# A chunked RWKV-7 recurrence with a SoLU block: all chunk products on 64x64 blocks, paired evictions, two-block solve hops, and another order of loads

## The chip, the core and the metric

The kernel runs on one core of one Trainium2 chip. The metric is the device time of one execution in microseconds (us), lower is better. The core has TensorE (PE, matrix products, writes to PSUM only), VectorE (DVE), ScalarE (ACT), GpSimd (POOL) and SyncE (SP); SP and ACT, and in the changed kernel POOL too, issue DMA transfers. "PEld" in the profile is the weight load of TensorE.

## The reference

Two blocks follow one another. The first is a recurrence for 4 batches of 8 heads, 768 tokens and head width 40; the second is a feed-forward block on the result (3072 tokens of width 320).

```python
for t in range(S):                                   # per batch and head; state is 40 x 40
    y[t]  = r[t] @ state
    Sa    = state @ a[t]
    state = state * w[t][None, :] - outer(Sa, b[t]) + outer(v[t], k[t])
x  = y laid out as (batch, token) x (head, width)    # 3072 x 320
h  = x @ w_in                                        # 320 x 1024
e  = exp(h - max(h)); solu = h * e / (sum(e) + 1e-9)
ln = (solu - mean(solu)) / sqrt(var(solu) + 1e-6) * g_ln
out = ln @ w_out                                     # 1024 x 320
```

The recurrence's inputs are fp32. `w_in` and `w_out` arrive as 64-bit floats, which the kernel loads as pairs of 32-bit words and narrows to fp32 itself.

## The kernel before

**Tiling.** The 768 tokens are cut into chunks of 64. A step `i` of the main loop handles chunk `i // 2` of batch pair `i % 2`, so there are 24 steps; a tile has 128 partitions, 64 tokens of each of the two batches. Within a step a "unit" (p, g, q, h) is one batch half `p` and one head, given by three bits. Most products are made per unit, 16 of them, on 64 x 64 blocks of the PE array; `in_turn` deals the units over the blocks in turn, so that neighbours in the instruction stream use different blocks. A fp32 product shows as two records in the profile.

**What a step does.** `decay` takes the logarithm of `w` (`lw`), sums it over the chunk by products with a triangle (`pcum`, `pex`), and scales `b` and `k` (`kb`, on POOL, then to DRAM as `kb_dram`). `front` transposes `b` and `a` (`pbT`, `paT`; four 128-wide transposes each) to `bT` and `aT`. `norm` makes the strictly triangular matrix `nt` of each unit, and `spread` writes its 32 x 32 diagonal blocks, by way of DRAM, into a tile `blk` in which four steps fill the 128 partitions. `invert` inverts these blocks on DVE for four steps at once: 30 substitution steps of two operations (`prod`, `uu`), each dependent on the one before; it is a generator, from which `some(n)` draws at several places of the loop. `bring` loads the inverses as `tu` and `uh`. `couple` (product `py`, then `wy`) and `close` (product `pz`) make the off-diagonal block of the 64 x 64 inverse: the two hops of the solve. `attend` transposes `k`, `v`, `r` (`pkT`, `pvT`, `prT`), `states` the state (`psT`); each transposition is evicted by an ACT copy of its own. `scores` (`ps`) makes the masked tiles `psi` and `lv` of the next step on DVE. `carried` and `driven` (`px`) make the right-hand side, `solved` (`pu`) the solution, `answered` (`pl`) the masked tile `lu`, `read` (`pyo`) the outputs and the state's increment, `leave` the scaled outputs `x` (sent through DMA into `xT`) and the new state. The feed-forward block follows: `hidden` (`h`, its maximum `nmax`, the exponential `e`), `weighed`, `spreadof` (`bs`, `mv`, `c`, `rs`), `folded` (`plnT`) and `output` (`po`, `osb`).

**Order.** The loop (L660 to 704) runs the stages of different steps beside each other: in pass `i`, `decay` belongs to step i + 9, `front` to i + 8, `norm` to i + 7, `attend`, `couple`, `scores` and `close` to i + 1, `carried` to `leave` to i, `hidden` to i - 1 and `output` to i - 2. PE executes in the order in which the loop writes its instructions. The order on the other engines is decided by a scheduler when the kernel is built, from its own estimate of when each operand is ready; on the chip each engine then runs its list strictly in order. PSUM is used through a ring of six one-bank tiles (`bank`) and one two-bank tile for `h`; a new bank waits until the readers of the tile six places earlier are done.

**Weights.** `weights` is a generator from which the passes -4 to 0 draw. Its loads are issued from ACT's queue into two alternating tiles (`landing`), and each piece is narrowed by `narrow`: three operations on DVE for the bits, a clamp and the last product on POOL (L143, L152), two conversions on ACT (L144, L147) and two more operations on DVE (L149, L150). `w_out` pieces are also scaled by `g_ln` on POOL (L184); then a product `pmean` and a subtraction centre them.

Of the kernel before, what the change touches and what calls it, by code (L numbers as in the profile page):

```python
# [16 lines left out]
P = 128  # L17
# [28 lines left out]
def kernel(  # L46
# [34 lines left out]
    ps1 = ctx.enter_context(tc.tile_pool(name="ps1", bufs=6, space=PSUM))  # L81
    ps2 = ctx.enter_context(tc.tile_pool(name="ps2", bufs=1, space=PSUM))
    ctx.enter_context(tc.manual_schedule(engines={mybir.EngineType.PE}))
# [24 lines left out]
    a_t = zeroed(nc.vector, "a", [P, H, C], 3, pad)  # L108
# [5 lines left out]
    r_t = zeroed(nc.gpsimd, "r", [P, H, C], 2, pad)  # L114
    v_t = zeroed(nc.gpsimd, "v", [P, H, C], 2, pad)
# [12 lines left out]
    def bank(name):  # L128
        return ps1.tile([P, 512], FP32, tag="bank", name=name)


    def narrow(dst, bits):
# [4 lines left out]
        def tmp(name):  # L137
            return two.tile([P, 512], I32, tag=name, name="n_" + name)[0:n, 0:width]

        man, scale, low = tmp("psi"), tmp("s"), tmp("rT")  # L140
        ts = nc.vector.tensor_scalar
        ts(out=scale, in0=hi, scalar1=20, scalar2=0x7FF, op0=ALU.logical_shift_right, op1=ALU.bitwise_and)
        nc.gpsimd.tensor_scalar(out=scale, in0=scale, scalar1=1023 - 127, scalar2=1023 + 128, op0=ALU.max, op1=ALU.min)  # L143
# [8 lines left out]
        nc.gpsimd.tensor_tensor(out=dst, in0=frac, in1=scale.bitcast(FP32), op=ALU.mult)  # L152

    landing = ["e", "lnT"]

    def load_weight(dst, parts, step):
        n, width = dst.shape
        wide_ = parts[0].dtype != FP32
        to = dst
        if wide_:  # L160
            landing.reverse()
            to = two.tile([P, 512], I64, tag=landing[0], name="bits", bufs=1)[0:n, 0:width]
        row = 0
        for part in parts:
            nc.scalar.dma_start(out=to[row:row + part.shape[0]], in_=part)
            row += part.shape[0]
        yield
        if wide_:
            for lo in range(0, width, step):
                narrow(dst[:, lo:lo + step], to[:, lo:lo + step])  # L170
                yield

    def weights():
        nc.scalar.dma_start(out=g_rows, in_=moe_g_ln.rearrange("(c p) -> c p", p=P))
        for cols in (slice(0, 512), slice(512, 1024)):
            for kt in range(NK):
                yield from load_weight(w_in[0:D * len(TILE_HEADS[kt]), kt, cols],
                                       [moe_w_in[h * D:h * D + D, cols] for h in TILE_HEADS[kt]], 256)
        pg = bank("pg")
        nc.tensor.transpose(out=pg[:, 0:NF], in_=g_rows, identity=ident[0:NF, 0:NF])  # L180
        nc.scalar.copy(out=g_col, in_=pg[:, 0:NF])
        for c in range(NF):
            yield from load_weight(w2[:, c, :], [moe_w_out[c * P:(c + 1) * P, :]], DM)
            nc.gpsimd.tensor_scalar(out=w2[:, c], in0=w2[:, c], scalar1=g_col[:, c:c + 1],  # L184
                                    scalar2=None, op0=ALU.mult)
        t = bank("pmean")
        for c in range(NF):
            nc.tensor.matmul(t[:, 0:DM], lhsT=c_("mean"), rhs=w2[:, c, :], start=c == 0, stop=c == NF - 1)
        nc.vector.tensor_tensor(out=w2, in0=w2, in1=t[:, 0:DM].unsqueeze(1).to_broadcast([P, NF, DM]),
                                op=ALU.subtract)  # L190
        yield
# [8 lines left out]
    units = [(p, g, q, h) for g in range(2) for p in range(2) for q in range(2) for h in range(2)]  # L200
# [16 lines left out]
    def pair(t, j):  # L217
        return t[:, j:j + 2, :].rearrange("p a b -> p (a b)")[:, 0:W2]
# [10 lines left out]
    def load(x, ap, i):  # L229
        bp, ci = where_(i)  # L230
        for p in range(2):
            nc.sync.dma_start(out=x[half(p), :, 0:D],
# [6 lines left out]
    def load_keys(i):  # L239
# [3 lines left out]
        for n, ap in (("w", w), ("b", b), ("k", k), ("a", a)):  # L243
            x = a_t[i % 3] if n == "a" else two.tile([P, H, D], FP32, tag="raw_" + n, name="raw_" + n)
            d["raw_" + n] = x
            load(x, ap, i)

    def load_values(i):
# [3 lines left out]
        for n, ap in (("v", v), ("r", r)):  # L252
            d["raw_" + n] = two.tile([P, H, D], FP32, tag="raw_" + n, name="raw_" + n)
            load(d["raw_" + n], ap, i)

    def in_value_order(i):
        if not ok(i):
            return
        d = st[i]
        d["v"], d["r"] = v_t[i % 2], r_t[i % 2]  # L260
        d["lv"] = two.tile([P, H, W2], FP32, tag="lv", name="lv")
        for x, n in ((d["v"][:, :, 0:D], "raw_v"), (d["r"][:, :, 0:D], "raw_r"), (d["lv"][:, :, C:], "raw_v")):
            nc.gpsimd.tensor_copy(out=x.rearrange("p (h x) d -> p h x d", h=2),  # L263
                                  in_=d[n].rearrange("p (x h) d -> p h x d", h=2))


    def decay(i):
# [5 lines left out]
        t = bank("pcum")  # L273
        nc.tensor.matmul(heads(t[:, 0:DM]), lhsT=c_("cum"), rhs=lw[:, :, 0:D], start=True, stop=True)  # L274
        inv = two.tile([P, DM], FP32, tag="inv", name="inv", bufs=1)
        nc.scalar.activation(out=inv, in_=t[:, 0:DM], func=AF.Exp, scale=-1.0)  # L276
        t = bank("pex")
        for j in range(4):
            nc.tensor.matmul(t[0:W2, j * P:(j + 1) * P], lhsT=pair(lw, 2 * j), rhs=c_("cum"), start=True, stop=True)  # L279
        ex = d["ex"] = ex_t[i % (AHEAD + 3)]  # L280
        nc.scalar.activation(out=ex[0:W2, :, :, 1:].rearrange("p b j t -> p j b t"),
                             in_=t[0:W2].rearrange("p (j b t) -> p j b t", j=4, b=2), func=AF.Exp)
# [5 lines left out]
    def turned(name, src_, bufs=1, evict=True):  # L288
        t = bank("p" + name)
        for j in range(4):  # L290
            nc.tensor.transpose(out=t[0:W2, j * P:(j + 1) * P], in_=pair(src_, 2 * j), identity=ident)  # L291
        if not evict:
            return t
        o = two.tile([P, 4, P], FP32, tag=name, name=name, bufs=bufs)
        nc.scalar.copy(out=o[0:W2].rearrange("p j t -> p (j t)"), in_=t[0:W2])
        return o

    def front(i):
        if not ok(i):
# [3 lines left out]
        ex = d["ex"]  # L303
        d["bT"] = turned("bT", d["kbw"][:, H:, :])
        t = turned("aT", d["raw_a"], evict=False)
        aT = d["aT"] = two.tile([P, 4, P], FP32, tag="aT", name="aT", bufs=AHEAD + 2)
        nc.vector.tensor_tensor(out=aT[0:W2].rearrange("p j (b t) -> p j b t", b=2),
                                in0=t[0:W2].rearrange("p (j b t) -> p j b t", j=4, b=2),
                                in1=ex[0:W2, :, :, 0:C].rearrange("p b j t -> p j b t"), op=ALU.mult)

    def masked(dst, t):
        nc.vector.tensor_tensor(out=dst, in0=t, in1=tri.unsqueeze(1).to_broadcast([P, 4, C]), op=ALU.mult)  # L312

    def keyed(t, i, u):
        p, g, q, h = u
        return t[rows(h), 2 * g + q, p * C:p * C + C]

    def valued(t, i, u):
        p, g, q, h = u
        return t[rows(q), 2 * h + g, p * C:p * C + C]  # L320

    def norm(i):
# [3 lines left out]
        t = [bank("pnt") for _ in range(2)]  # L326
        for u in in_turn(lambda p, g, q, h: (h, p ^ h)):
            p, g, q, h = u
            j = 2 * g + q
            mm(t[h][half(p ^ h), j * C:j * C + C], keyed(d["bT"], i, u), keyed(d["aT"], i, u))  # L330
        nt = d["nt"] = two.tile([P, 2, 4, C], FP32, tag="nt", name="nt", bufs=AHEAD + 1)
        for h in range(2):
            masked(nt[:, h], t[h][:, 0:256].rearrange("p (j c) -> p j c", j=4))
        d["nt_dram"] = dram.tile([P, H, C], FP32, tag="nt_dram", name="nt_dram", bufs=3)
# [35 lines left out]
    def bring(i):  # L370
# [6 lines left out]
        for x in range(2):  # L377
# [4 lines left out]
            nc.sync.dma_start(out=d["uh"][hi],  # L382
                              in_=uu[at + 16 + 8 * x:at + 24 + 8 * x, :, Q:].rearrange("h s t -> s h t"))

    def fetch(i):
# [3 lines left out]
        d["kb"] = two.tile([P, 2 * H, C], FP32, tag="kbx", name="kbx")  # L389
        nc.sync.dma_start(out=d["kb"], in_=d["kb_dram"])  # L390

    def couple(i):
# [3 lines left out]
        t = [bank("py") for _ in range(2)]  # L396
        for u in in_turn(lambda p, g, q, h: p ^ h):
            p, g, q, h = u
            j, x = 2 * g + q, half(p ^ h)
            mm(t[h][x, j * Q:j * Q + Q], d["nt"][x, h, j], d["tu"][x, 4 * h + j, 0:Q])  # L400
        for h in range(2):
            nc.scalar.activation(out=wy[:, h, :, 0:Q], in_=t[h][:, 0:4 * Q].rearrange("p (j c) -> p j c", j=4),
                                 func=AF.Copy, scale=c_("neg_hi"))

    def close(i):
# [3 lines left out]
        t = [bank("pz") for _ in range(2)]  # L409
        for u in in_turn(lambda p, g, q, h: p ^ h):  # L410
            p, g, q, h = u
            j, x = 2 * g + q, half(p ^ h)
            mm(t[h][x, j * Q:j * Q + Q], wy[x, h, j], d["uh"][x, 4 * h + j])
# [321 lines left out]
```

## Time and profile before

| what | value |
|---|---|
| time, median of 3 runs | 818.68 us (818.12 to 820.93) |
| the profiled execution | 821.3 us, span from first to last instruction 819.5 us |
| mean granted TensorE clock | 0.863 of full speed |
| busy: PE, weight loads, DVE, ACT, POOL | 644.9, 480.8, 379.0, 239.8, 168.4 us |
| DMA | 84.31 MB in 224901 packets, 103 GB/s on average |
| `pu` of step 0, of step 2, of step 23 start at | 157.6, 206.6, 778.5 us |

The times in lines of the profile are microseconds from the start of the span. A busy engine is not necessarily the one that sets the end; the chain of waits and the timeline say which one does at a given place. The profiled execution is one run, and it took 2.6 us more than the median.

### The profile page before, as it was taken

Reading aid. Unit: us, or ns where it says so; the run is one execution under the profiler, and the core shown is the slowest. Engines: PE = TensorE matmul, PEld = TensorE weight load, DVE = VectorE, ACT = ScalarE, POOL = GpSimd, SP = SyncE. Lnnn points to the kernel's source line nnn. Section 1 sums busy time; section 2 is a strip of 40 time slices with the busy share of each in tenths; the row PEclk is TensorE's granted clock in tenths of the full one; section 3 lists DMA queues with packets and bytes.
Section 4 is the critical chain, followed back from the end, with each engine's and each line's share of the span. In section 5 each row is a group of like instructions: output and inputs, shape, how many; then the busy total and the mean of one; then the engine's idle time right before and its main releaser. Section 6 shows DMA issues by size and latency. Waiting matters only on the chain.

```text
span 819.5 us, 26810 instructions
## 1 busy us (share of the span) xinstructions
PE 644.9 (79%) x11545; PEld 480.8 (59%) x11545; DVE 379.0 (46%) x1048; ACT 239.8 (29%) x592; POOL 168.4 (21%) x237
## 2 busy tenths in 40 slices
PE   4505506778989989889889899798997877989894
PEld 3304404657757766667667667676765665666652
DVE  3563572478403692343954228822479133123322
ACT  3323102323324322433234334133321222223121
POOL 6664234313202211221022102301111110000000
PEclk8655756669989989999989999799997789899997
DMA  7546847364464545554625655265422412011000
GB/s 149 145 133 138 204 109 191 64 138 95 96 169 108 111 79 129 155 122 89 146 80 115 152 133 127 49 161 125 97 70 52 120 47 54 23 52 41 15 20 13
DMA packets 224901, 84.31 MB, mean 103 GB/s; under 512 B 206088, under 2 KB 213136, under 8 KB 224016
## 3 DMA queue, kind: packets, MB, share of 16 engines
q1 hardware_dynamic: 220272, 76.12, 40.4%
q10 hardware_dynamic: 4512, 6.48, 2.7%
q8 instruction: 91, 1.49, 0.7%
q14 instruction: 26, 0.21, 0.1%
HBM read 49.53 MB, written 29.10 MB: 96 GB/s over the span
## 4 chain that ended last, share of the span: by engine, by line
PE 46%; DVE 23%; DMA 15%; issue 5%; POOL 5%; ACT 3%; SPq 2%; ACTq 0%; DVEq 0%; POOLq 0%
PE h L592 14%; PE po L642 10%; DMA kbx<-kb_dram 7%; DVE prod L360 5%; DVE uu L362 5%; PE pz L211 3%; PE pyo L211 3%; DVE e L604 3%; DVE nmax L595 3%; PE py L211 3%; DVE bs L612 2%; DMA uu_dram<-uu 2%; PE pu L211 2%; POOL n_s L143 2%; ACT e L598 2%
## 5 line engine op out<-in xcount | busy, mean ns | idle before, releaser
L595 DVE TENSOR_REDUCE nmax<-h 128x1 f32<-128x1024 f32 x24 | 29.4, 1223 | 305.0 <-PE h L592 305.0
L592 PE MATMUL h<-w_in,xT 120*128 120x512 f32 (+1 forms) x288 | 135.8, 622 | 0.0
L642 PE MATMUL po<-w,lnT 128*128 128x320 f32 x384 | 115.4, 456 | 3.9 <-ACT lnT L633 3.9
L642 PEld LDWEIGHTS po<-w,lnT 128*128 128x128 f32 x384 | 75.7, 203 | 34.9 <-ACT lnT L633 5.4
L592 PEld LDWEIGHTS h<-w_in,xT 120*128 120x128 f32 (+1 forms) x288 | 55.0, 197 | 62.2 <-issue 61.1
L598 ACT ACTIVATE e<-h,nmax 128x1024 f32<-128x1024 f32 x24 | 26.8, 1116 | 147.5 <-DVE nmax L595 147.5
L360 DVE TENSOR_TENSOR prod<-blk,uu 128x30 f32<-128x30 f32 (+9 forms) x180 | 62.9, 350 | 6.0
L362 DVE TENSOR_TENSOR uu<-uu,prod 128x30 f32<-128x30 f32 (+9 forms) x180 | 61.5, 342 | 5.7
L291 PE MATMUL pkT<-cst,kbx 128*104 128x128 f32 x96 | 18.7, 330 | 45.5 <-DMA kbx<-kb_dram 42.7
L621 POOL TENSOR_TENSOR rs<-c,mhalf 128x1 f32<-128x1 f32 x24 | 13.4, 557 | 188.7 <-DVE c L620 135.6
L285 POOL TENSOR_TENSOR kb<-raw_b,inv 128x320 f32<-128x320 f32 x24 | 20.9, 869 | 151.4 <-ACT inv L276 131.1
L291 PE MATMUL pbT<-cst,kb 128*104 128x128 f32 x96 | 18.4, 323 | 39.5 <-POOL kb L285 39.5
L263 POOL COPY v<-raw_v 128x320 f32<-128x320 f32 x24 | 10.9, 456 | 179.8 <-DMA raw_v<-in_v_dram 179.7
L274 PE MATMUL pcum<-lw,cst 128*128 128x320 f32 x48 | 24.6, 605 | 24.6 <-ACT lw L272 14.7
L211 PE MATMUL pyo<-lv,kbx 64*64 64x104 f32 x768 | 42.2, 268 | 0.5 <-DVE lv L312 0.4
L211 PE MATMUL pyo<-lu,kbx 64*64 64x104 f32 x768 | 41.0, 261 | 0.8 <-DVE lu L312 0.5
L291 PEld LDWEIGHTS pkT<-cst,kbx 128*104 128x104 f32 x96 | 12.2, 154 | 50.0 <-issue 46.9
L644 ACT ACTIVATE osb<-po,rs 128x320 f32<-128x320 f32 x24 | 12.7, 527 | 94.5 <-PE po L642 94.5
L211 PE MATMUL py<-tu,nt 64*64 64x32 f32 x768 | 30.6, 227 | 8.2 <-DMA tu<-uu_dram 6.0
L279 PEld LDWEIGHTS pex<-cst,lw 128*104 128x104 f32 x192 | 32.8, 223 | 7.0 <-issue 4.1
L474 ACT COPY x<-px 128x160 f32<-128x160 f32 x48 | 11.7, 295 | 83.7 <-PE plnT L632 25.4
L291 PEld LDWEIGHTS pbT<-cst,kb 128*104 128x104 f32 x96 | 11.4, 149 | 41.8 <-POOL kb L285 40.5
(105 smaller groups left out, 1253.1 us busy)
## 6 DMA issues: line engine op xcount, KB each, us to landing
kb_dram<-kb SPq DMA_DIRECT2D x24, 512.0 KB
kbx<-kb_dram SPq DMA_DIRECT2D x24, 512.0 KB
nt_dram<-nt SPq DMA_DIRECT2D x24, 256.0 KB
uu_dram<-uu SPq DMA_DIRECT2D x6, 1024.0 KB
raw_w<-in_w_dram SPq DMA_DIRECT2D x48, 80.0 KB
raw_b<-in_b_dram SPq DMA_DIRECT2D x48, 80.0 KB
raw_k<-in_k_dram SPq DMA_DIRECT2D x48, 80.0 KB
a<-in_a_dram SPq DMA_DIRECT2D x48, 80.0 KB
```

Of the source, the lines that this page charges most:

```text
L211: nc.tensor.matmul(o, lhsT=lhsT, rhs=rhs, start=start, stop=stop, skip_group_check=True)
L274: nc.tensor.matmul(heads(t[:, 0:DM]), lhsT=c_("cum"), rhs=lw[:, :, 0:D], start=True, stop=True)
L279: nc.tensor.matmul(t[0:W2, j * P:(j + 1) * P], lhsT=pair(lw, 2 * j), rhs=c_("cum"), start=True, stop=True)
L285: nc.gpsimd.tensor_tensor(out=kb[:, j * H:j * H + H, 0:D], in0=d["raw_" + n], in1=heads(inv), op=ALU.mult)
L291: nc.tensor.transpose(out=t[0:W2, j * P:(j + 1) * P], in_=pair(src_, 2 * j), identity=ident)
L360: nc.vector.tensor_tensor(out=t, in0=nb[:, j:j + 1, j + 1:Q].to_broadcast([P, j, m]), in1=u[:, 0:j, j:j + 1].to_broadcast([P, j, m]), op=A ...
L362: nc.vector.tensor_tensor(out=u[:, 0:j, j + 1:Q], in0=u[:, 0:j, j + 1:Q], in1=t, op=ALU.subtract)
L592: nc.tensor.matmul(h[:, hh], lhsT=d["xT"][0:n, kt, :], rhs=w_in[0:n, kt, hh], start=kt == 0, stop=kt == NK - 1)
L595: nc.vector.tensor_reduce(out=nmax, in_=h, axis=AX.X, op=ALU.max, negate=True)
L598: nc.scalar.activation(out=e, in_=h, func=AF.Exp, bias=nmax, accum_out=d["esum"])
L604: nc.vector.tensor_tensor(out=d["e"], in0=d["h"], in1=d["e"], op=ALU.mult)
L642: nc.tensor.matmul(o[:, 0:DM], lhsT=d["lnT"][:, f, :], rhs=w2[:, f, :], start=f == 0, stop=f == NF - 1)
```

## The change

- Every product of the recurrence now uses 64 x 64 blocks. The transpositions `paT`, `pbT`, `pkT`, `pvT`, `prT`, `psT`, and the sums `pcum` and `pex`, are made per unit as products with a 64 x 64 identity or triangle. Results of two transpositions share a tile and are evicted together (`pkv` to `kv`, `prs` to `rs`); `states` is merged into `attend`.
- The hops `py` and `pz` put their results in other halves of the partitions, so that the units use all four blocks rather than two.
- PSUM is a ring of three two-bank tiles (`banks`). Masks, `nuT`, `lu`, `x0` and `tot` are each made by one operation over both banks.
- `v` and `r` are loaded directly to where they are used; the three POOL copies of `in_value_order` go. `nt` is no longer kept in SBUF from `norm` to `couple` but fetched again from DRAM (`ntx`). `kbx` has three buffers, the raw tiles three, `a` four.
- POOL's instructions, like PE's, stay in the order in which they are written.
- The loads of the first four steps are issued before the loop, those of `k` and `a` from ACT's queue. `w_in` is loaded from SP's queue and narrowed on DVE and ACT in pass 0; `w_out` is loaded from POOL's queue and narrowed in pass 1, with the clamp and the products on POOL.
- The loop's order is another: `front` and `decay` come after `driven`, `output` before `solved`, `attend` and `couple` before `hidden`, and `answered` and `scores` after `spreadof`.

```diff
-    ps1 = ctx.enter_context(tc.tile_pool(name="ps1", bufs=6, space=PSUM))
+    ps1 = ctx.enter_context(tc.tile_pool(name="ps1", bufs=3, space=PSUM))
-    ctx.enter_context(tc.manual_schedule(engines={mybir.EngineType.PE}))
+    ctx.enter_context(tc.manual_schedule(engines={mybir.EngineType.PE, mybir.EngineType.Pool}))
...
+    def make_w2():
+        pg = banks("pg")[:, 0]
...
         for c in range(NF):
-            yield from load_weight(w2[:, c, :], [moe_w_out[c * P:(c + 1) * P, :]], DM)
+            to = w2[:, c]
+            if moe_w_out.dtype != FP32:
+                to = two.tile([P, DM], I64, tag=("e", "lnT")[c % 2], name="bits", bufs=1)
+            nc.gpsimd.dma_start(out=to, in_=moe_w_out[c * P:(c + 1) * P, :])
+            if moe_w_out.dtype != FP32:
+                narrow(w2[:, c], to, nc.gpsimd)
             nc.gpsimd.tensor_scalar(out=w2[:, c], in0=w2[:, c], scalar1=g_col[:, c:c + 1],
                                     scalar2=None, op0=ALU.mult)
...
+    def turn(t, to, of, at, x):
+        mm(t[half(to), of, at:at + C], x, ident[half(of), half(of)])
+
+    def turned(t, at, src_, keys):
+        for u in in_turn(lambda p, q, g, h: (p, h if keys else q)):
+            p, q, g, h = u
+            j = at + (2 * q + g if keys else 2 * g + h)
+            turn(t, h if keys else q, p, j * C, src_[half(p), head(u)])
+        return t[0:W2, :, at * C:at * C + 4 * C].rearrange("p b (j t) -> p b j t", j=4)
...
-            nc.tensor.transpose(out=t[0:W2, j * P:(j + 1) * P], in_=pair(src_, 2 * j), identity=ident)
...
     def fetch(i):
-        d["kb"] = two.tile([P, 2 * H, C], FP32, tag="kbx", name="kbx")
+        d["kb"] = two.tile([P, 2 * H, C], FP32, tag="kbx", name="kbx", bufs=3)
         nc.sync.dma_start(out=d["kb"], in_=d["kb_dram"])
+        d["nt"] = tokens("ntx", 2)
+        nc.sync.dma_start(out=d["nt"].rearrange("p h j c -> p (h j) c"), in_=d["nt_dram"])
...
     def couple(i):
-        for u in in_turn(lambda p, g, q, h: p ^ h):
-            mm(t[h][x, j * Q:j * Q + Q], d["nt"][x, h, j], d["tu"][x, 4 * h + j, 0:Q])
+        for u in in_turn(lambda p, q, g, h: (p ^ h, p)):
+            mm(t[half(p), h, j * Q:j * Q + Q], d["nt"][x, h, j], d["tu"][x, 4 * h + j, 0:Q])
```

The new loop, without the stages' guards:

```python
    for i in range(3):
        load_keys(i)
    for i in range(first, N + 2):              # first = -9, j = i + 7
        if i == 0: make_w_in()
        if i == 1: make_w2()
        carried(i); driven(i); norm(j); spread(j)
        # every fourth pass: start invert(n), some(1)
        front(j + 1); decay(j + 2); load_keys(j + 5)
        if j == -1: fetch_w_in()
        some(3)
        if i == 2: centre_w2()
        folded(i - 2); output(i - 2); load_values(i + 2); fetch(i + 2); some(3)
        solved(i); couple(i + 1); attend(i + 1)
        hidden(i - 1); weighed(i - 1); spreadof(i - 1); some(3)
        decay_turned(j + 2); answered(i); scores(i + 1); some(3)
        close(i + 1); read(i, True); read(i, False); leave(i)
        # every fourth pass: some(40)
        bring(i + 2)
```

## The prediction

> **What bounds the kernel now.** I read the page's chain first, then the chain in order of time, then one undisturbed chunk engine by engine, then waits, clock and the weight conversion. The chain by engine:
>
> ```profile
> PE 46%; DVE 23%; DMA 15%; issue 5%; POOL 5%; ACT 3%; SPq 2%; ACTq 0%; DVEq 0%; POOLq 0%
> ```
>
> TensorE (PE) leads, but half of the chain is elsewhere. The chain in order of time (start, length, what) gives the stages, because `nmax` runs once per chunk right after `h`:
>
> ```profile
> 137.87 3.29 DMA bits<-in_moe_w_out_dram
> ...
> 214.06 1.24 DVE nmax L595
> ...
> 655.68 1.24 DVE nmax L595
> ...
> 800.73 1.23 DVE nmax L595
> ```
>
> So the start (to `nmax` of chunk 1) takes 214 us, sixteen chunks take 441.6 (27.6 each), the last six 145, the end 18.8. The start is weight conversion: a `w_out` piece lands 3.3 us after its issue. Next, PE in one undisturbed chunk (430 to 455 us; start, length, x = records, two per fp32 matmul):
>
> ```profile
> 430.88 1.11 PE L211 MATMUL py<-tu,nt 64*64 64x32 f32 x32
> 431.92 5.42 PE L592 MATMUL h<-w_in,xT 120*128 120x512 f32 x12
> 437.79 0.65 PE L211 MATMUL ps<-aT,kT 40*64 40x64 f32 x32
> 439.31 0.60 PE L291 MATMUL paT<-cst,a 128*104 128x128 f32 x4
> 440.29 1.04 PE L279 MATMUL pex<-cst,lw 128*104 128x128 f32 x8
> 443.79 1.07 PE L211 MATMUL pz<-uh,wy 64*64 64x32 f32 x28 [0.23 <-DVE c L618]
> ```
>
> PE hardly waits here. By start-to-start distance `py`, on two 64x64 blocks, costs 1.04 us; `ps`, as many records over four blocks, 0.47. After `h` PE has 6.5 us of other work, while VectorE (DVE) and ScalarE do this:
>
> ```profile
> 437.38 1.23 DVE L595 TENSOR_REDUCE nmax<-h 128x1 f32<-128x1024 f32 x1 [15.30 <-PE h L592]
> 438.64 1.12 ACT L598 ACTIVATE e<-h,nmax 128x1024 f32<-128x1024 f32 x1 [3.85 <-DVE nmax L595]
> 439.88 1.23 DVE L604 TENSOR_TENSOR e<-h,e 128x1024 f32<-128x1024 f32 x1 [0.61 <-ACT e L598]
> 441.68 0.74 DVE L312 TENSOR_TENSOR lv<-ps,cst 128x256 f32<-128x256 f32 x2
> 442.34 1.27 DVE L612 BATCH_NORM_STATS2 bs<-e 128x6 f32<-128x512 f32 x2
> ```
>
> The mask `lv` comes before the statistics `bs`, 5.2 us after `h`. The difference between 25.1 us of this chunk and the mean of 27.6 is the inversion (every fourth chunk, about 29.5) and the wait for `kbx`:
>
> ```profile
> PE pkT L291 <- DMA kbx<-kb_dram: 42.7, 17, 13.5
> ```
>
> Waits also cost clock (window, PE busy, and the granted clock PEclk):
>
> ```profile
> 196.00:198.00 2.00, 0.71 (x52) 0.59 (x41) 1.90 (x9) 0.00 (x0) 0.00 (x0) 1.00 0.94 170
> 198.00:200.00 2.00, 1.58 (x8) 1.61 (x9) 1.97 (x7) 0.02 (x1) 0.74 (x1) 0.56 0.94 370
> ```
>
> One gap of 1.7 us was followed by 3 us at about half clock. The `w_out` conversion, from the groups by shape (busy us, mean ns):
>
> ```profile
> L143 POOL TENSOR_SCALAR n_s<-n_s 128x320 int32<-128x320 int32 x8 | 10.5, 1314 | 2.2 <-DVE n_s L142 1.6
> L184 POOL TENSOR_SCALAR w<-w,g_col 128x320 f32<-128x320 f32 x8 | 9.0, 1137 | 5.3 <-ACT g_col L181 4.9
> L152 POOL TENSOR_TENSOR w<-n_psi,n_s 128x320 f32<-128x320 f32 x8 | 7.1, 890 | 6.3 <-DVE n_psi L149 3.6 <-DVE n_s L150 2.6
> ```
>
> **Matmuls.** A transposition becomes sixteen plain 64x64 products instead of four 128-wide transposes. The row of `paT` steps in 0.44 to 0.48 us; the nearest row for the new form is `ps`, 0.47: nothing gained or lost. The Trainium skill, "TensorEngine Tiling (Array Packing)", Feature Incompatibilities, speaks against the change: column tiling excludes the fp32 transpose mode. The trace shows that mode's worth: `pex`, a plain product of the same shape as `paT`, takes 0.88. Four blocks at once buy back what the mode gave, so rule and rows price it at zero. `py` and `pz` go from 1.04 and 0.85 to 0.45 each (floor: `px`, 0.44 for 32 records); `pex` from 0.88 to 0.50; `psT` from 0.58 to 0.48. Together 1.5 us per chunk less PE. `pcum` stays at 0.54.
>
> **The new order after `h`.** The built order, not the diff, shows the cost. DVE now runs `nmax`, `lu`, `e`, `bs` twice, `psi`, `lv`; PE runs `pex`, `pl`, `ps`, `pz`, all of `pyo`, then `px` of the next chunk. `px` needs `psi` and `lv`, and its PSUM pair is the one `ps` held. DVE from the end of `h`: `nmax` to 1.3, exponential, `e` to 3.8, `bs` to 5.1, `psi` 5.8, `c` and `mv` between, `lv` 6.6; with a hand-over 6.7. (A masked 512-wide operation is taken at 0.68, the `aT` row's.) PE by then has 0.5 + 0.5 + 1.0 + 0.5 + 0.5 (`pyo` from the state) + 1.85 = 4.9 us of work, so it idles 1.8. Behind the waiting `px` stand `pnt`, the transpositions, `pcum`, `plnT`, `po`, `pu`, `h`: 0.8 + 0.45 + 0.5 + 0.95 + 0.55 + 1.05 + 4.4 + 0.95 + 0.45 + 1.9 + 5.35 = 17.3. A clean chunk is 24.0. The 1.8 us gap costs clock between 0 (gaps of 1.2 us at 255 and 606 us did nothing) and 1.6 (the 1.7 us gap above); I take 1.0, hence 25.0. The skill's "TensorE: Matmul & The Clock Gate", Part 1, puts the loss only at about 3.4 us of idle; by it this term is 0 and clean chunks cost 24.0, but the row above contradicts it.
>
> **The inversion.** Its 60 operations are now placed behind `lv`, before and between `x`, `tot`, `nt` and `aT`; before, 47 of them filled DVE's idle time under `po` and `h`. Nine small ones and a 0.72 copy delay `x` by 3.2 us, four more `nt`, six `aT`. The PSUM pairs of `pyo`, `pnt` and `pa` come free by these, so PE stalls 3.5 us before `pa` and 2.3 before `po`, and clock costs about 3 more: 33 us for each of four such chunks (29.5 before). Sixteen chunks: 12 x 25.0 + 4 x 33 = 432, rounded up to 436 for uncounted `tu` waits (6.0 us before): -6. Bounds: 24.0/30 gives 408 (-34); 26.5/37 gives 466 (+24).
>
> **`kbx`, DMAs, evictions.** A third `kbx` buffer lets the fetch go before `pyo`; its wait goes, and `ntx` (256 KB per chunk, two steps ahead) and two more `uh` issues (0.45 us each) fit SP's queue: about 16 us of issues in a 24 us chunk, all of `xT` still 11 us ahead of `h`. ScalarE's paired evictions (1.1 us) lie under `h`. The three POOL copies (0.46 each) were hidden already: zero. What is late next is DVE's `lv`.
>
> **The last six chunks** have no front work: 24.0 - 2.0 + 1.3 for clock = 23.3, five times, plus 16: 132.5, -12 (bounds -20, 0).
>
> **The start.** `w_in` moves its POOL steps (1.2 us each) to DVE, and DVE meets ten of its pieces before the third `nt`. A piece is a chain of 142, 143, ScalarE, 150, 152: 2.45 us; ten from 27.5 (their last loads leave SP at 22 to 26) end at 52. Four more fronts at 6 to 8 us each put the first inversion at 77 (before 93); 24 us of it, copy 1.95, `uu_dram` 4, `tu` 3 and 14 from `py` to `pu` put `pu` of chunk 0 at 125 (before 157.6). But POOL is now in written order, and the whole `w_out` conversion stands behind chunk 0's state update, at 141. The load of each piece stands on POOL behind the last step of the piece before, so nothing overlaps: 3.3 + 0.32 + 1.31 + 0.47 + 0.52 + 0.89 + 1.14 + hand-overs 0.3 = 8.3 us. The first piece also stands on DVE behind 34 inversion operations, and ends near 166; seven more end at 224. `x` and `tot` of chunk 1 on DVE, and `kb`, `rs` and the state update on POOL, wait behind it, and `pa` on PE for `kb`. Then `kb` 1.8, transpositions and `pcum` 3, `pmean` 7 on a cold clock, subtraction 2.8, `po` 4.4: `pu` of chunk 2 at 243 instead of 206.6: +37. Bounds: pieces at 4.3 us, the pace of the overlapped pieces at 134 to 150 us, +9; pieces at 9.5 with a front 5 us later, +50. A DMA issued from POOL does not occur in the trace; its row is ScalarE's. The skill's "DMA: Bandwidth & Descriptors" gives that path about 0.4 us more first-byte latency, which would add 3 us by an estimate from that page.
>
> **Sum.** 819.5 + 37 - 6 - 12 = 838.5 us of span, +19. The profiled execution was 821.3 us, 2.6 above the median of 818.7; on the median +19 is 838.
>
> **Rivals.** (1) Faster: the serial start is cheaper. With -18 from the rest, it must lose less than 18, which means a piece under (206.6 + 18 - 17 - 166) / 7 = 5.9 us. The row at 137.87 (landing hidden behind the piece before) speaks for it; POOL's written order, which forbids exactly that, against. At 4.3 us: 819.5 + 9 - 18 = 810, median 810. (2) Slower still: the 1.8 us gap drops the clock in every chunk for 5 to 6 us instead of 3, as after the waits at 234 and 301 us. Then chunks cost 26.5 and 37, the loop +24 and the tail 0: 819.5 + 37 + 24 = 880. Against it: the 1.2 us gaps that cost nothing. (3) No change, that the small products do not run four at a time: PE then keeps its 1.5 us per chunk, and terms cancel near 819 only by chance.
>
> **How the numbers follow.** Forecast 0.50, (1) 0.24, (2) 0.22, (3) 0.04. Anything within 0.3%, 2.5 us, cannot be told from no change here. Faster 0.23, same 0.04, slower 0.73. The forecast's own bounds are 815 to 862; the range reaches to (1) and most of the way to (2): 806 to 876.
>
> **What would show it.** Right: eight `w_out` pieces 8 to 9 us apart between 145 and 230 us, `pu` of chunk 2 near 243; PE waiting for DVE before `px` by 1.5 to 2 us in clean chunks; no wait for `kbx`; `py` and `pz` at 0.45. Wrong: `pu` of chunk 2 before 225, a clean chunk over 26.5, or inversion chunks no longer than 29.

## The result and the profile after

The changed kernel takes 887.55 us (median; 882.3 to 897.97) against 818.44 us of the kernel before beside it: ratio 1.0816, 95% interval 1.0760 to 1.0872. (Ratios here and below leave disturbed runs out; medians do not.) The forecast was 838, the range 806 to 876: the direction was right, the size was not. The profiled execution took 882.3 us with a span of 880.5, so 61 us of span have to be found; the forecast had found 19 of them.

The stages first, by the starts of `nmax`, as in the prediction. The changed kernel's run at 252.25 (chunk 1), 715.99 (chunk 17) and 861.00 us (chunk 23):

| stage | before | forecast | after |
|---|---|---|---|
| start, to chunk 1 | 214.1 | +37 | 252.3 (+38.2) |
| sixteen chunks | 441.6 | -6 | 463.7 (+22.1) |
| last six | 145.1 | -12 | 145.0 (0) |
| end | 18.8 | 0 | 19.5 (+0.7) |

The start is right to about 1 us. Of the miss of 42 us, 40 lie in the loop and its tail. The chain by engine says of what kind it is:

```profile
PE 44%; DVE 19%; DMA 12%; issue 11%; ACT 4%; POOL 4%; SPq 3%; ACTq 1%; DVEq 0%; POOLq 0%
```

"issue", time in which an engine waited for nothing that the profile shows, has gone from 5% to 11%. PE's waits in the loop alone (252 to 716 us; us in total, times, longest) name the places:

```profile
PE plnT L644 <- ACT lnT L645: 16.3, 16, 3.0
PE prs L217 <- issue: 14.3, 10, 2.1
PE pa L217 <- DVE tot L586: 9.1, 7, 3.2
PE pyo L217 <- issue: 7.3, 7, 2.3
PE pz L217 <- issue: 6.8, 4, 3.3
PE px L217 <- issue: 5.3, 7, 1.3
...
PE px L217 <- DVE psi L325: 1.7, 4, 0.8
```

Two kinds of wait stand here that the prediction does not have, `plnT` for ScalarE and "issue"; the one that it has in every chunk, `px` for VectorE, is all but missing. (`pa` for `tot` is the stall that it forecast for the inversion.) `plnT` waits for ScalarE, because both halves of its result now share one PSUM tile: the second half's transposes wait for the eviction of the first. And PE stops in the middle of runs of small products. On PE's timeline (start, length, x = records; in brackets the idle time before):

```profile
407.16 0.31 PE L217 MATMUL pyo<-lv,kbx 64*64 64x104 f32 x3 [2.31 <-issue]
...
444.29 0.66 PE L644 MATMUL plnT<-cst,e 128*128 128x128 f32 x4 [0.73 <-ACT lnT L645]
...
450.15 0.65 PE L217 MATMUL py<-tu,ntx 64*64 64x32 f32 x32
450.61 0.67 PE L217 MATMUL pkv<-cst,kbx 64*64 64x64 f32 x32
...
452.04 0.52 PE L217 MATMUL prs<-cst,st 64*64 64x64 f32 x23
453.74 0.38 PE L217 MATMUL prs<-cst,st 64*64 64x64 f32 x9 [1.18 <-issue]
```

`py` takes 0.46 us to the next start, as forecast. But a transposition, 32 records long, is cut after 23 of them, although all its operands are there. The page has the reason in two places, the busy line and the DMA queues:

```profile
PE 617.2 (70%) x16145; PEld 450.5 (51%) x16145; DVE 369.2 (42%) x907; ACT 226.7 (26%) x426; POOL 121.6 (14%) x173
```

```profile
q8 instruction: 127, 2.08, 0.9%
```

PE runs 16145 matmul records and as many weight loads, 32290 instructions (23090 before). Queue 8, of the kind "instruction", brings 127 packets, 2.08 MB, so 16 KB and one packet for 254 of PE's instructions each (91 packets before, again one for 254). So it is read as PE's own supply. The trace supports that: in the list of PE's instructions, with the few semaphore waits among them counted, the waits named "issue" stand at a fixed distance. All 34 of them in the loop, 40.1 us, come at the same place of every 256 instructions (before: 4 of 6, 1.3 of 1.7 us). In the whole run they are 46 and 49.7 us (before: 7 and 3.6), and each of the 46 ends 2.2 to 3.1 us after the transfer of a 16 KB packet began. (The expectations below count these gaps about from one instruction's start to the next one's start: 49 gaps, 56.6 us.) PE runs through 256 instructions of small products in about 1.9 us (four groups of 32 records at 0.46 to 0.50 us each), and the next packet isn't there.

### The profile page after: what moved, and what is told of

The parts are those of the page before. It is cut to its first block, busy times and chain, and to the rows that moved or that the text cites. A ratio compares the mean times of both kernels' runs of the same rounds, so it can differ in the third digit from the quotient of the medians.

```text
span 880.5 us, 35557 instructions
## 1 busy us (share of the span) xinstructions
PE 617.2 (70%) x16145; PEld 450.5 (51%) x16145; DVE 369.2 (42%) x907; ACT 226.7 (26%) x426; POOL 121.6 (14%) x173
## 3 DMA queue, kind: packets, MB, share of 16 engines
q8 instruction: 127, 2.08, 0.9%
## 4 chain that ended last, share of the span: by engine, by line
PE 44%; DVE 19%; DMA 12%; issue 11%; ACT 4%; POOL 4%; SPq 3%; ACTq 1%; DVEq 0%; POOLq 0%
PE h L604 12%; PE po L654 11%; DVE uu L375 3%; DVE prod L373 3%; DMA bits<-in_moe_w_out_dram 3%; PE plnT L644 3%; PE pyo L217 2%; PE prs L217 2%; PE pkv L217 2%; PE pu L217 2%; DVE e L616 2%; DVE bs L624 2%; PE pa L217 2%; DVE x L572 2%; SPq L239 2%
## 5 line engine op out<-in xcount | busy, mean ns | idle before, releaser
L604 PE MATMUL h<-w_in,xT 120*128 120x512 f32 (+1 forms) x288 | 131.9, 607 | 0.2 <-issue 0.2
L654 PE MATMUL po<-w,lnT 128*128 128x320 f32 x384 | 125.4, 486 | 1.7 <-DVE w L196 1.2
L217 PE MATMUL pa<-cst,kb 64*64 64x64 f32 x768 | 23.3, 266 | 61.0 <-POOL kb L277 56.2
L644 PE MATMUL plnT<-cst,e 128*128 128x128 f32 x192 | 38.0, 330 | 39.4 <-ACT lnT L645 33.0
L644 PEld LDWEIGHTS plnT<-cst,e 128*128 128x128 f32 x192 | 24.4, 163 | 55.6 <-ACT lnT L645 39.5
L217 PEld LDWEIGHTS pa<-cst,kb 64*64 64x64 f32 x768 | 20.2, 176 | 62.6 <-POOL kb L277 57.3
L217 PE MATMUL py<-tu,ntx 64*64 64x32 f32 x768 | 18.3, 228 | 40.1 <-DMA tu<-uu_dram 40.0
L505 ACT COPY x<-px 128x320 f32<-128x320 f32 x24 | 10.2, 424 | 137.1 <-issue 44.3
L610 ACT ACTIVATE e<-h,nmax 128x1024 f32<-128x1024 f32 x24 | 26.7, 1113 | 58.4 <-DVE nmax L607 57.8
L645 ACT COPY lnT<-plnT 128x512 f32<-128x512 f32 x48 | 28.1, 586 | 36.6 <-PE plnT L644 32.8
L322 DVE TENSOR_TENSOR aT<-pa,ex 104x512 f32<-104x512 f32 x24 | 16.5, 689 | 50.0 <-ACT bT L309 50.0
L217 PEld LDWEIGHTS py<-tu,ntx 64*64 64x64 f32 x768 | 15.7, 145 | 41.9 <-issue 39.0
```

What stands on the lines that cost most here:

```text
L217: nc.tensor.matmul(o, lhsT=lhsT, rhs=rhs, start=start, stop=stop, skip_group_check=True)
L604: nc.tensor.matmul(h[:, hh], lhsT=d["xT"][0:n, kt, :], rhs=w_in[0:n, kt, hh], start=kt == 0, stop=kt == NK - 1)
L610: nc.scalar.activation(out=e, in_=h, func=AF.Exp, bias=nmax, accum_out=d["esum"])
L644: nc.tensor.transpose(out=t[:, x, j * P:(j + 1) * P], in_=d["e"][:, f * P:(f + 1) * P], identity=ident)
L645: nc.scalar.copy(out=lnT[:, x * (NF // 2):(x + 1) * (NF // 2)].rearrange("p f t -> p (f t)"), in_=t[:, x])
L654: nc.tensor.matmul(o[:, 0:DM], lhsT=d["lnT"][:, f, :], rhs=w2[:, f, :], start=f == 0, stop=f == NF - 1)
```

## The experiments

**The supply by itself.** Nothing of the computation is left but PE with three streams of independent products over four 64x64 blocks.

```diff
+    def stream(name, count, width):
+        t = ps1.tile([P, 2, 512], FP32, tag="banks", name=name)
+        for n in range(count):
+            p, x, at = n % 2, n // 2 % 2, n // 4 % 2 * 64
+            nc.tensor.matmul(t[half(x), p, at:at + width], lhsT=ident[half(p), half(p)], rhs=cst[half(p), 0:width],
+                             start=True, stop=True, skip_group_check=True)
...
+    stream("p_64", 768, 64)
...
+    stream("p_96", 768, 96)
...
+    stream("p_160", 768, 160)
```

> No part of the computation: PE alone runs three streams of 768 independent 64x64 fp32 products over four blocks, with 64, 96 and 160 moving columns, each after 160 128-wide transposes, and zeros are written as the output. 768 products are 3072 PE instructions, twelve blocks of 256. Theory A (a block of 256 instructions is supplied in 3.2 to 3.4 us, whatever it contains): with 64 columns (1.87 us of array time per block) a gap of 1.3 to 1.5 us at every 256th instruction, stream of about 40 us instead of 22; with 96 columns (2.8 us) gaps of about 0.5 us; with 160 (4.7 us) none. Theory B (gaps come from semaphores or from the other queues of the full kernel): no gaps in any of the three.

PE's timeline of that run:

```profile
22.70 3.02 PE L120 MATMUL p<-cst 64*64 64x64 f32 x191
26.70 2.09 PE L120 MATMUL p<-cst 64*64 64x64 f32 x128 [0.98 <-issue]
30.43 2.09 PE L120 MATMUL p<-cst 64*64 64x64 f32 x128 [1.64 <-issue]
34.43 2.09 PE L120 MATMUL p<-cst 64*64 64x64 f32 x128 [1.91 <-issue]
...
89.70 2.87 PE L120 MATMUL p<-cst 64*64 64x96 f32 x128 [0.86 <-issue]
93.16 2.87 PE L120 MATMUL p<-cst 64*64 64x96 f32 x128 [0.59 <-issue]
...
142.20 18.02 PE L120 MATMUL p<-cst 64*64 64x160 f32 x524
```

Every row is 128 records with their 128 loads, 256 instructions, and then PE stops. With 64 columns ten such blocks take 37.01 us (26.70 to 63.71), 3.70 each; with 96 columns nine take 32.73, 3.64 each, though the products are longer; with 160 columns, 4.4 us per block by the row, nothing stops. So a block is supplied in about 3.7 us with either width (the expectation had 3.2 to 3.4), and only what lasts longer hides it. The first 191 records run without a gap: what is ahead when this dense stretch begins covers one to two blocks. Theory A holds; semaphores, other queues and traffic are not needed for it.

The Trainium skill, "Runtime: NRT & Kernel Launch", Instruction fetch mechanics, has the block of 256 instructions, as the trace does. It also says that fetching is mostly hidden because engines issue more slowly than blocks arrive; PE's 7.3 ns per instruction in these streams is the case in which that fails, and the measurement decides here.

**The same instructions in another order.** One chunk has 1345 PE instructions on the mean, nearly all in small products that stand in two dense stretches: 416 records from `pex` to `pa` (the expectation's 480 counts `pyo` too high) and 224 from `pu` to `prs`. The next run adds and drops nothing; it makes `h`, `plnT` and `po` give way after their first halves and puts small products between (`turns` is `plnT`, `written` is `po`).

```diff
-        folded(i - 2)
-        output(i - 2)
+        next(written, None)
...
+        shown = hidden(i - 1)
+        next(shown, None)
         attend(i + 1)
-        hidden(i - 1)
+        next(shown, None)
...
         read(i, True)
+        turns, written = folded(i - 1), output(i - 1)
+        next(turns, None)
         read(i, False)
+        next(turns, None)
+        next(written, None)
```

> The changed kernel with not one instruction added or taken away, only PE's order changed: h in two halves with the transpositions of k, v, r and the state between them, plnT's halves on both sides of the second half of pyo, po in two halves, one before px and one after pcum. The 480 records of small products that stood in one dense stretch are split by long matmuls. Theory A (supply of instructions): a block of 256 PE instructions that lasts over 3.3 us shows no gap; gaps fall from 56.6 to under 25 us, and the wait of plnT for ScalarE from 33 to under 15: 840 to 860. Theory B (the number of products, or VectorE's chain, sets the time wherever they stand): within 10 us of 887.

Measured: 838.78 us, 1.0215 (1.012 to 1.031), so 49 us less than the changed kernel. The loop takes 437.8 and the tail 126.9; the prediction's sum had 436 and 132.5 for them. PE's waits in that loop (253 to 691 us):

```profile
PE pz L217 <- issue: 9.7, 5, 3.2
PE pyo L217 <- DVE lu L325: 9.6, 4, 6.6
PE pyo L217 <- issue: 8.4, 6, 2.6
...
PE plnT L646 <- DVE c L632: 1.9, 5, 0.6
```

`prs` and the wait of `plnT` for ScalarE have left the list; `issue` is 21.5 us in all, and `pyo` now waits 9.6 us for VectorE. The run changes several places at once, so the next ones take it apart.

**Its parts.** First, `plnT` alone:

```diff
-        t = banks("plnT")
         for x in range(2):
+            t = banks("plnT")[:, 0]
```

> The changed kernel, with the two halves of plnT in two PSUM pairs instead of one. In the changed kernel the second half's transposes wait 24 times, 33.0 us in all, for ScalarE to evict the first half. Theory A (that wait is on the path): it goes, and po waits in its place for the same eviction by 0.2 to 0.4 us per chunk, so 887.5 falls by 15 to 28 us, to 860 to 873. Theory B (the loop is bound elsewhere, the wait is filled by what comes after it): within 4 us of 887.5.

Measured 884.59 (1.0763; 1.0654 to 1.0872): B by its number. The wait for the eviction is gone (5.3 us of other waits stay at `plnT`), but `issue` in the loop rises from 40.1 to 44.7 us, `po` waits for the same eviction (3.1 us in the loop, 9.5 in the run), and 41 us of clock are lost in the loop instead of 32. The rise of `issue` suggests that PE had used part of that wait to be supplied.

Second, `h` alone, in the two lines for `hidden` and `attend` above:

> The changed kernel with one thing moved on PE: the first half of h (six records) goes before the transpositions of k, v, r and the state, the second half stays behind them. Nothing is added; plnT, po and pyo stand where they stood. Theory A (supply of instructions alone, without the plnT wait): the gaps before prs (15.5 us) and part of those before pkv and pz go, 10 to 20 us: 868 to 878, plnT's wait for ScalarE stays at about 33. Theory B (the gain of the spread-out order came from plnT's wait and from po before px, not from supply): within 4 us of 887.

Measured 888.7 (1.0836; 1.0789 to 1.0884). B by its number. The gaps before `prs` did go, as A said, and `issue` in the loop fell to 29.3 us, but the mean clock of the run was 0.82 against 0.855, and the loop lost 55 us to it instead of 32, more than the gaps gave.

Third, all of the spread order except the split of `h`:

> The spread-out order without its split of h: k, v, r and the state are transposed before all of h again; plnT's halves and the halves of po stand as in the spread-out order. h split alone brought nothing (888.7). Theory A (the gain is in the place of po's first half, which gives PE something sparse to do between the dense stretches before and after px, and in plnT's halves): 838 to 850. Theory B (all three splits are needed, since gaps move to the next dense stretch): 855 to 875.

Measured 855.25 (1.045; 1.0356 to 1.0544), loop 443.4, tail 131.9: 32 of the 49 us without the split of `h`, which is worth the other 16 here and nothing by itself. B's number.

**Is it PE's supply or VectorE's chain?** In the spread order `po` also stands where VectorE works from `h` to `lv`, which the prediction took for the limit. Three runs separate the two. Only VectorE's order:

```diff
-        spreadof(i - 1)
         some(3)
         decay_turned(j + 2)
         answered(i)
         scores(i + 1)
+        spreadof(i - 1)
```

> The changed kernel with only VectorE's order changed: bs and mv are recorded after the masks psi and lv. Theory A (PE's supply of instructions sets the pace, gaps before pz and pyo cover VectorE's chain from h to lv): within 5 us of 887. Theory B (the chain h, nmax, e, bs, psi, lv, px sets the period, and PE's gaps only fill its slack): 1.3 us per chunk less, 855 to 870.

Measured 890.28 (1.0795; 1.0714 to 1.0876): A. `plnT` and `po` moved there whole:

```diff
+        folded(i - 2)
+        output(i - 2)
         carried(i)
         driven(i)
...
-        folded(i - 2)
-        output(i - 2)
```

> The changed kernel with plnT and po, both whole, moved on PE from behind pcum to between pyo and px. Counted by blocks of 256 instructions with 3.3 us each, this order leaves as many gaps as the changed kernel's (3.8 against 3.9 us per chunk), while po now stands where VectorE works from h to lv. Theory A (supply): as many gaps, plnT's wait for ScalarE stays, within 8 us of 887. Theory B (VectorE's chain): 850 to 868.

Measured 901.68 (1.0946; 1.085 to 1.1042): slower than both theories said, and B is out. With `po` gone from between them, `pnt` to `prs` are one dense stretch, and `issue` in the loop is 57.8 us; the count of blocks had not said so. Last, both single edits that had brought nothing:

> The changed kernel with both edits that brought nothing alone: h in two halves round the transpositions, and plnT in two PSUM pairs. By the same count of blocks the gaps fall from 3.9 to 2.9 us per chunk and plnT's 0.75 us wait goes; po stays behind pcum. Theory A: the two add up once the clock is even, 855 to 872. Theory B (PE's waits between px and h are not what sets the period): 880 or more.

Measured 870.52 (1.0561; 1.0474 to 1.0648): A. Together they bring 17 us. The table puts the loops side by side. "Counted" is an estimate of the gaps per chunk from PE's order alone: every group at its own row's time, cut into blocks of 256 instructions, 3.3 us at least for a block. "Issue" is PE's idle time of that name in the loop, "plnT" all other idle time before `plnT` there; the lost clock is the loop's time times what PEclk lacks.

| order | counted x 16 | issue | issue + plnT | lost clock | loop | tail | median |
|---|---|---|---|---|---|---|---|
| before | | 1.7 | 1.7 | 27 | 441.6 | 145.1 | 818.4 |
| changed | 62 | 40.1 | 58.0 | 32 | 463.7 | 145.0 | 887.6 |
| after_bs | 62 | 48.1 | 66.2 | 43 | 472.6 | 145.3 | 890.3 |
| po_first | 61 | 57.8 | 69.5 | 46 | 495.8 | 138.6 | 901.7 |
| two_plnT | 63 | 44.7 | 50.0 | 41 | 468.7 | 142.1 | 884.6 |
| h_split | 45 | 29.3 | 48.8 | 55 | 467.9 | 146.0 | 888.7 |
| h_and_plnT | 46 | 33.6 | 37.5 | 34 | 451.8 | 139.7 | 870.5 |
| spread_no_h | 45 | 30.0 | 31.9 | 24 | 443.4 | 131.9 | 855.3 |
| spread_out | 28 | 21.5 | 23.3 | 24 | 437.8 | 126.9 | 838.8 |

The count is too high, since other waits stretch blocks too, but apart from po_first it is so by nearly the same factor (`issue` is 0.65 to 0.78 of it). From spread_out to changed the two waits grow by 34.7 us and the loop by 25.9. h_and_plnT, spread_no_h and after_bs lie within 4 us of that line; two_plnT and h_split lie 11 us above it and po_first 23, and these three lost 9 to 22 us more to the clock than changed did. But after_bs lost 10 more as well, and in po_first `po` waits another 10.0 us for ScalarE. So the waits order the loops, and what the clock costs besides is not separated.

The tail is another matter. Between 716 and 861 us of the changed kernel `issue` is 5.7 us, and `plnT` waits longer:

```profile
PE plnT L644 <- ACT lnT L645: 15.3, 6, 3.0
```

Yet two_plnT, without that wait, has a tail only 3 us shorter, while the two orders that also move `po` bring it to 131.9 and 126.9. What of them does it was not taken apart.

**Fewer instructions.**

```diff
-    def turned(t, at, src_, keys):
...
+    def turned(t, at, src_, adjacent):
+        s = at // 4
+        for j in range(4):
+            to = t[:, s, j * P:(j + 1) * P]
+            if adjacent:
+                nc.tensor.transpose(out=to, in_=src_[:, 2 * j:2 * j + 2].rearrange("p a b -> p (a b)"), identity=ident)
+            else:
+                for q in range(2):
+                    mm(to[half(q)], src_[:, 4 * q + j], ident)
```

> The changed kernel, with five of its six transpositions per chunk made again of four 128-wide fp32 transposes, and the sixth (v) of eight products of 128x64 tiles; results land in the same places, r is loaded by two more DMAs per chunk. Instructions of PE per chunk fall by about 270 of 1345. Theory A (PE runs out of instructions: 49 gaps after instruction 192 of every 256, 56.6 us in all after 260 us): most of these gaps go, 30 to 45 us, less 10 us for the slower form of v: 850 to 868, and fewer than 25 such gaps. Theory B (the small products cost nothing in supply, and the loss is in the order of VectorE): 887 plus 10, and as many gaps in PE, with other names.

Measured 892.38 (880.12 to 898.85, no interval). Records fall from 16145 to 12457, the "issue" waits at the fixed place from 46 to 24 in the run and from 40.1 to 24.9 us in the loop (all `issue` there: 33.2 us). But the form for `v` takes 1.02 us instead of 0.46, a 128-wide transposition among 64x64 products 0.44 to 0.59, and 44 us of clock are lost in the loop instead of 32. Inconclusive: fewer gaps, as A said, no gain.

**The start.** The load of each `w_out` piece issued one piece ahead:

```diff
-        for c in range(NF):
+        def landed(c):
...
+        ahead = landed(0)
+        for c in range(NF):
+            to, ahead = ahead, landed(c + 1) if c + 1 < NF else None
```

> The changed kernel, with the load of each w_out piece issued from POOL before the POOL steps of the piece before it, instead of after them. Theory A (the start is lost because a landing of about 3.2 us stands in series with each of eight pieces): seven landings go under the 5 us of POOL steps, pieces come 5.0 to 5.5 us apart instead of 8.2, nmax of chunk 1 is at 227 to 232 us instead of 252, and the time is 862 to 868. Theory B (POOL steps and the queue behind them set the pace): pieces still over 7 us apart, time over 880.

Measured 866.58 (1.06; 1.0511 to 1.0688): A. POOL's timeline has the issues 5.2 to 6.1 us apart, where the changed kernel has 8 to 9:

```profile
172.37 0.59 POOL L186 DMA_DIRECT2D bits<-in_moe_w_out_dram  x1
...
177.60 0.59 POOL L186 DMA_DIRECT2D bits<-in_moe_w_out_dram  x1
```

`nmax` of chunk 1 comes at 231.0 instead of 252.3. With the spread order the two gains add:

> The spread-out order with each w_out load issued one piece ahead. The start and the loop are separate stages, so the two gains should add: 838.8 - 21 = 818 (813 to 823), nmax of chunk 1 at 230, loop 438, tail 127. If both gains come from the same wait, over 830.

Measured 822.81 (1.0032; 0.9988 to 1.0075), `nmax` of chunk 1 at 234.5, loop 440.2, tail 127.2: they add. Then the place of the conversion itself (`make_w2()` one chunk earlier):

> The same with the whole w_out conversion recorded one chunk earlier, before chunk 0 instead of before chunk 1: on POOL it then stands behind kb of chunk 8 and in front of chunk 0's state update, and runs while the first inverse travels to its place (from about 103 us). Theory A (the start was lost by the place of the conversion in POOL's written order): eight pieces of about 5 us end near 145, lu of chunk 0 waits on VectorE behind them until then, pu of chunk 1 follows near 170, nmax of chunk 1 is at 185 to 205 instead of 230, and the time is 775 to 795, less than the kernel before. Theory B (chunks 0 and 1 wait for something else, the inverse or w_in): nmax of chunk 1 still over 215, time over 805.

Measured 814.01 (0.9923; 0.9889 to 0.9957), `nmax` of chunk 1 at 226.3: B by its numbers, though not by the cause that it names. The pieces run from 106 to 160 us and do not end near 145, and `wy` of chunk 1 now stands on ScalarE behind them: `pex` waits 19.4 us for it. Two more edits on top, VectorE's order and the two POOL steps of each piece on VectorE:

> The same, with the statistics of e (bs, mv) recorded after the masks psi and lv, as in the kernel before. Built, VectorE runs one bs, psi, lv, then the other bs. The prediction had counted a wait of 1.8 us per chunk of px for lv behind bs. Theory A (that wait is real, but covered by po before px and by gaps of supply): within 4 us of the run without this edit. Theory B (VectorE's order costs 1 to 2 us per chunk): 20 to 40 us less.

> The early w_out conversion with its two POOL steps per piece (1.29 and 0.87 us) on VectorE, as w_in has them; only the factor g stays on POOL. In the run with the steps on POOL eight pieces took from 106 to 160 us, 5.3 us apart, and wy of chunk 1 and lu of chunk 0 stood behind them until 157 and 159. VectorE needs 2.5 us per piece and the two landing buffers allow one per 3.2 us: pieces end near 135, nmax of chunk 1 is 20 to 25 us earlier (about 203), time 788 to 796. If the inverse of the second group is late instead: over 805.

The first measured 813.63 (0.979; 0.9731 to 0.9848): A's number by the median, but by the ratio, against 0.9923 without the edit, about 11 us less, between A and B. Its tail is 120.3 instead of 127.3, its loop no shorter (441.7 against 434.2): with the supply relieved, VectorE's order does count where there is no front work. The second measured 810.7 (0.9878; 0.9798 to 0.9957): `nmax` of chunk 1 at 219.0, not 203, and the time over 805. Its pieces end at 154, not near 135; one load, issued 1.7 us behind another, took 8.05 us to land where the expectation had 3.2. Last, both together with `pa` in 128-wide transposes:

> The same, with bs after the masks and the two transpositions of pa (a and b) again as 128-wide transposes: 56 records of 672 per chunk go, all from the dense stretch after px. Theory A (supply): the gaps before pa, pnt and pcum shrink, 3 to 10 us less than the run without it. Theory B: within 3 us of it.

Measured 803.79 (0.9747; 0.9659 to 0.9835), the lowest median here and 18 us under that of the kernel before beside it; the interval overlaps that of the run with VectorE's order alone. What `pa` adds cannot be told from VectorE's order in this run: its tail, 120.0, is the same.

## Why the prediction was wrong

**The start: right.** Pieces 8 to 9 us apart, `pu` of chunk 0 at 124.1 (forecast 125), `pu` of chunk 2 where it was forecast, at 243, in the chain in order of time:

```profile
178.74 2.99 DMA bits<-in_moe_w_out_dram
...
186.65 3.15 DMA bits<-in_moe_w_out_dram
...
219.70 3.17 DMA bits<-in_moe_w_out_dram
...
243.43 1.07 PE pu L217 x64
```

The mechanism is shown: w_out_ahead takes out what overlaps, 21 us. That the number fits to 1 us is partly luck: the last piece ended at 226.8, not 224, and what follows took 16.6 us where the sum had 19. (Rival (1) counts 17 for that stretch; with the 19 of the sum its limit for a piece is 5.7 us, not 5.9.)

**Matmuls: the step that failed is "rule and rows price it at zero".** In array time it is right (0.46 to 0.50 us per transposition, in a stretch without a gap), and so are `py` and `pz`; only `pcum` takes 0.69 us and not 0.54. But four transposes are 8 PE instructions and sixteen products 64; six transpositions and `pex` add 384 to the 962 of a chunk. The prediction read records as time and never as instructions to be brought; that term, left at zero, is the `issue` of the loop, 40.1 us where before had 1.7. With the inversion's four chunks set apart, the other twelve took 28.4 us on average and not 25.0. The row to look at was on the page of before: queue 8, 91 packets, one per 9 us on average. The page doesn't say how fast it can go, but in the trace of before no two of these packets start less than 3.43 us apart (3.23 in the changed kernel, 3.44 in the stream), and 7 waits stand at the fixed place.

**`plnT`: missed.** The tiles of two banks were costed by their evictions only. That the shared tile also makes the second half of `plnT` wait for the eviction of the first, 0.7 us in most chunks and up to 3.0 in the tail, was to be read from the diff. The wait is real, but taken out alone it brought 3 us, within the scatter of the runs; with the supply relieved too, by the split of `h`, the two brought 17.

**The inversion: sized too high.** The four chunks that hold it took 28.3 to 33.6 us, 30.8 on average, and not 33: `pa` waits 9.1 us for `tot` in the whole loop, not 3.5 in each of four chunks. So the clean chunks missed by more than the loop did.

**The wait of `px` for `lv`: real in kind, not in place.** VectorE does run both `bs` before `psi` and `lv`, and `lv` ends some 6.4 us after `h`, as forecast. But PE came to `px` late, by gaps in `pz` and `pyo` (2.31 us in the rows above), so `px` waits 1.7 us in the whole loop and not 1.8 per chunk. after_bs shows that the term is empty here.

**The clock: nearly the right size, by other waits.** The prediction charged the loop with about 24 us (1.0 in each of twelve chunks, 3 in each of four), for gaps before `px`, `pa` and `po` that came smaller or not at all; so the fit is luck. PEclk in the loop is 0.93, 32 us lost (before 0.94 and 27); the rows by stretch, after and then before:

```profile
252.00:716.00 464.00, 387.57 (x10519) 281.05 (x10521) 209.71 (x500) 133.65 (x241) 51.61 (x76) 0.93 0.45 110
```

```profile
214.00:656.00 442.00, 396.10 (x7695) 297.76 (x7698) 219.82 (x611) 142.18 (x355) 73.51 (x114) 0.94 0.48 113
```

PE is busy 8.5 us less, where the prediction had 1.5 per chunk, in a loop 22 us longer. Rival (2) has nearly the right time, 880, for a wrong reason: its drop of the clock in every chunk did not come. The prediction's own sign, a clean chunk over 26.5 us, did (26.85 us from 401.77 to 428.62). `kbx` no longer waits, as forecast.

**Open:** why h_split, two_plnT, after_bs and po_first lose 9 to 22 us more to the clock than the changed kernel, and what makes up the 12.5 us by which the tail is longer than forecast (VectorE's order is worth 7 us there with the supply relieved, and nothing in after_bs). That order of gaps, and not their sum, moves the clock is only argued.

## What to carry to other kernels

Count PE's instructions per stretch, not only its records' time: in the stream here 256 of them (128 small fp32 records with their loads) came every 3.45 to 4.00 us, so a dense stretch of 64x64 products longer than one or two such blocks stalls; long matmuls belong in the middle of such stretches, not behind them. When a removed wait brings nothing, look whether another took its time: two edits that were each worth nothing, or next to it, brought 17 us together. A tile that spans two PSUM banks can save an eviction, but it orders what is written to its halves: `plnT` waited 33.0 us for that here.

## What was not expected of the hardware

The stream with 64 columns stops for 1.4 to 1.9 us in every 3.7 and keeps a granted clock of 1.00 throughout, where the prediction had read half clock out of one gap of 1.7 us. The Trainium skill, "TensorE: Matmul & The Clock Gate", Part 1, with its loss only at about 3.4 us of idle, fits the stream; it does not fit the changed kernel's loop, where 3.4 us at half clock follow a gap of 2.07 us at 365 us. And the supply is not a constant: the blocks of that stream come 3.45, 3.73 or 4.00 us apart with nothing else on the DMA queues.
